# Values by seven products in the second layer of an attention and gated-unit kernel

## The chip, the cores and the metric

The kernel runs on one core of one Trainium2 chip. The metric is the time on the device in microseconds (us); the median over several executions counts. The engines are TensorE (PE, with its weight loads as PEld), VectorE (DVE), ScalarE (ACT), GpSimd (POOL) and SyncE (SP), which here only issues DMAs.

## The reference

Two layers, each a multi-head attention block and a gated linear unit, with the same weights in both. 2048 tokens, 448 features, 16 heads of 28, 1792 hidden features.

```python
def _A_ref(x, wqkv, wo):
    qkv = (x @ wqkv).reshape(B, S, 3, H, Dh).transpose(2, 0, 3, 1, 4)
    q, k, v = qkv[0], qkv[1], qkv[2]
    scores = einsum("bhqd,bhkd->bhqk", q, k) * (Dh ** -0.5)
    p = softmax(scores)
    o = einsum("bhqk,bhkd->bhqd", p, v)
    return o.transpose(0, 2, 1, 3).reshape(B, S, D) @ wo

def _B_ref(x, w_gate, w_up, w_down):
    return einsum("bsf,fd->bsd", sigmoid(x @ w_gate) * (x @ w_up), w_down)

x = A_x
x = x + _A_ref(_layernorm(x), A_wqkv, A_wo)
x = x + _B_ref(_layernorm(x), B_w_gate, B_w_up, B_w_down)
x = x + _A_ref(_layernorm(x), A_wqkv, A_wo)
x = x + _B_ref(_layernorm(x), B_w_gate, B_w_up, B_w_down)
```

## The kernel before, in words

Each layer runs four stages in a row: queries, keys and values (`project`), attention (`attend`), the output projection and the gated unit. The 2048 tokens are four blocks of 512, and a block is four tiles of 128. Numbers in single precision are split into a high and a low half-precision part, so that one exact product is three half-precision ones. The order on every engine is the order of the program text, for each engine by itself; waits are semaphores that the language puts in.

**Seven products.** In the second layer a block of activations stands in two halves each way, and products of 2 by 2 halves are made with seven products in place of eight: the activations' sums and differences lie in `blk.wide` (four operands) and `blk.short` (three, or four where the block keeps the eighth), the weights' sums in packs of 28 planes. Product k of operand k is five matmuls for k below 4 and six from 4 on. Products 0, 2, 3 and 5 are added up in one bank of PSUM (the chain), which is read after each of them; 1, 6 and 4 go to another bank (the side). Queries and keys (`qk_sums`) and the gate (`gate_and_up`) are made in this way. `split_sums` makes the 28 planes of a weight: four sums (`add_up`), four scaled high parts and four low parts on VectorE, then small copies on GpSimd.

**Values.** `vals` makes the values of a block tile by tile: `values_product` is 11 matmuls of 448 columns with the tile of activations as weights, and ScalarE or VectorE copies the bank out. In the second layer the order is: queries and keys of block 3 (`qk_sums(3, ...)`), values of block 2 (`vals(2, ...)`), values of tiles 0 and 1 of block 3, then a branch, tile 2 of block 3, and the first scores of attention. Tile 3 of block 3 is made between the first groups of scores (`last_values`).

**The guard and the branch.** `guard_of_norms` makes for each head a bound on its scores from the norms' maxima (`peaks`): VectorE, a root on GpSimd (L1245), and a scaled row of 2048 on VectorE that reads a cleared tile (`zero`, cleared at L1233). Two rows, the guard and the zeros, are stored to `g_scr` (L1249, L1250). `worst_of_heads` turns the bounds with a matmul (L1254) and compares the worst with a limit; all engines load the flag (L1262) and branch (L1263). The branch not taken holds a slow form (`true_maxima`). Behind it SP loads the guard of head 0 from `g_scr` (L801), which the first scores (L1559) read.

**Attention.** `attend` scores three units (128 keys by 512 queries) at a time into three banks (`score`), ScalarE makes the exponentials of the three in one instruction (L1574), and `mix` multiplies them with the values (L1609) some groups later. A few units of each head are scored aside (`score_aside`): VectorE makes their exponentials with a polynomial (L1584 to L1592). All aside scores of a head use the same bank of PSUM, so one waits until VectorE has read the one before. In the first layer `Prepare`, from step 4 on, reads the other weights, measures and splits them on VectorE and stores the parts (L1442), all DMAs on GpSimd's queue. At step 2 `keep` stores the split weights of queries, keys and values on SP's queue (L752).

**Buffers.** Large tiles in SBUF come from 19 equal buffers (`Slots`, `big`): `get` takes the one that has been free longest, `put` hands it back behind the others. The new user's first write waits until all uses of the old tile are over. `big.ring(6)` takes six for the exponentials.

```python
heads[0].load_guard()
heads[1].load()
heads[1].load_guard()
vals(3, blks[3], {}, [2], 0 if layer == 0 else 7)
```

These four lines stand behind the branch.

Of the kernel before, what the change touches and what calls it, by code (L numbers as in the profile page):

```python
# [59 lines left out]
DN = D // 2  # L60

# [66 lines left out]
def interleaved_layers(ctx: ExitStack, tc: tile.TileContext, x_in, wqkv, wo, w_gate, w_up,  # L128
# [92 lines left out]
    def load_rows(dst, src, c0, n, queue=nc.sync, second=None):  # L221

        for a, b in ((0, 2), (2, 3)) if second else ((0, 3),):
            (second if a else queue).dma_start(
                dst[:, a:b, :], src[a * P:b * P, c0:c0 + n].rearrange("(s p) n -> p s n", p=P))
        for r in (0, 64):
            (second or queue).dma_start(dst[r:r + 64, 3, :], src[384:448, c0:c0 + n])
# [30 lines left out]
    def add_up(v):  # L258

        s12, s34 = [qrt.get("sums", [P, 2, 2, P]) for _ in range(2)]  # L260
        l11, l12, l21, l22 = v[:, 0:2, 0], v[:, 2:4, 0], v[:, 0:2, 1], v[:, 2:4, 1]
        for to, a, b, op in ((s12[:, 0], l21, l22, ALU.add),
                             (s12[:, 1], s12[:, 0], l11, ALU.subtract),
                             (s34[:, 0], l11, l21, ALU.subtract),
                             (s34[:, 1], l12, s12[:, 1], ALU.subtract)):
            nc.vector.tensor_tensor(to, a, b, op=op)
        return s12, s34
# [383 lines left out]
    def of_halves(pm, w, blk, k, first):  # L651


        if k < 4:
            x = blk.wide[:, k]
            high, low, both = w(2 * k + 1), w(2 * k + 15), w(2 * k + 14)
            terms = [(high, x[:, 0, 1]), (high, x[:, 1, 1]), (low, x[:, 0, 1]),
                     (w(2 * k) if k else both, x[:, 0, 0]), (both, x[:, 1, 0])]
        else:
            x = blk.short[:, k - 4]  # L660
            terms = [(w(SHORT[k - 4][i]), x[:, j, 1 - t])
                     for t in range(2) for i, j in ((t, 0), (t, 1), (2 + t, 0))]
        for i, (a, x) in enumerate(terms):
            nc.tensor.matmul(pm, a, x, start=(first and i == 0),  # L664
                             stop=(i == len(terms) - 1), skip_group_check=True)

    def by_tokens(pm, hi, lo, tail, w, kts=range(4)):

        for kt in kts:
            if kt == 3:  # L670
                nc.tensor.matmul(pm, tail, w[:, 0, 3, :], start=False, stop=False)
                nc.tensor.matmul(pm, tail, w[:, 1, 3, :], start=False, stop=True)
                continue
            nc.tensor.matmul(pm, hi(kt), w[:, 0, kt, :], start=(kt == 0), stop=False)  # L674
            nc.tensor.matmul(pm, hi(kt), w[:, 1, kt, :], start=False, stop=False)  # L675
            nc.tensor.matmul(pm, lo(kt), w[:, 0, kt, :], start=False, stop=False)  # L676
# [3 lines left out]
    v_parts = dpool.tile([P, 2, 4, D], F16, name="v_parts")  # L680
    o_parts = dpool.tile([P, 2, 4, D], F16, name="o_parts")
# [5 lines left out]
    class WeightsQKV:  # L687
# [9 lines left out]
        def read(self, j):  # L697
            self.raw.append(big.get("wraw", [P, 4, D]))
            load_rows(self.raw[j], wqkv, j * D, D, second=None if j else nc.scalar)
# [45 lines left out]
        def split_v(self):  # L745
            for kts in (slice(0, 2), slice(2, 4)):
                scaled_split(self.v[:, 0, kts], self.v[:, 1, kts], self.raw[2][:, kts], 2)
            big.put(*self.raw)
# [12 lines left out]
        def load_rest(self):  # L761
# [3 lines left out]
            for i in range(2):  # L765
                nc.sync.dma_start(self.alone[i][:, 0:3], qk_parts[i, :, 0:3, c])
                r = slice(64 * i, 64 * i + 64)
                nc.sync.dma_start(self.alone[0][r, 3], qk_parts[i, r, 3, c])
                nc.sync.dma_start(self.v_tail[r], v_parts[r, i, 3])
# [51 lines left out]
    def project(layer, wq, begun):  # L821
# [10 lines left out]
        evac = [0]  # L832

# [271 lines left out]
        def values_product(pv, blk, j, kts=range(4)):  # L1105
            t = slice(j * P, (j + 1) * P)
            if blk.halves:
                c = slice(j % 2 * P, j % 2 * P + P)
                for s in kts:
# [7 lines left out]
                    for n, (i, w) in enumerate(((0, 0), (0, 1), (1, 0))):  # L1117
                        nc.tensor.matmul(pv[:, 0:D], x[:, i], wq.v[:, w, PLACES[r], :],  # L1118
# [3 lines left out]
                      blk.tail[:, t], wq.v, kts)  # L1122

        def vals(b, blk, after, tiles=range(TB), at=None, begun=None, banks=None):
# [14 lines left out]
            if tiles[-1] == TB - 1:  # L1139
                blk.drop()  # L1140

# [58 lines left out]
        else:  # L1200
            b2.clear()
            ones_of_values()
            b3.apart = True
# [11 lines left out]
                          None, True)  # L1215
            fin = qk_sums(3, b3, {}, fin)
# [14 lines left out]
        def guard_tiles():  # L1231
            tiles = [big.get(n, [H, S], F16) for n in ("guard", "zero")]
            nc.gpsimd.memset(tiles[1], 0.0)  # L1233
            return tiles

        guard_early = guard_tiles() if layer > 0 else None

        def guard_of_norms():
# [9 lines left out]
            queue = nc.gpsimd if guard_early else nc.sync  # L1248
            queue.dma_start(g_scr[:, 0, :], guard)  # L1249
            queue.dma_start(g_scr[:, 1, :], zero)  # L1250
# [8 lines left out]
        vals(2, blks[2], {layer: guard_of_norms, 3: worst_of_heads})  # L1259
        nc.scalar.activation(warm, warm, AF.Exp)  # L1260
        vals(3, blks[3], {}, range(2))
# [10 lines left out]
        vals(3, blks[3], {}, [2], 0 if layer == 0 else 7)  # L1272
# [258 lines left out]
    def attend(layer, values, heads, last_values, gate, wq):  # L1531
# [153 lines left out]
        begun = last_values()  # L1685

# [5 lines left out]
        for g in range(2, groups + 3):  # L1692
            more(g)
            if g == 2:
                last_values(begun)
            x = g - 2.25
# [621 lines left out]
```

## Time and profile before

| | |
|---|---|
| median of 3 runs | 1869.21 us (1868.77 to 1869.33) |
| profiled execution | 1869.45 us, span of its instructions 1867.7 us |
| busy | PE 100%, PEld 76%, DVE 78%, ACT 75%, POOL 16% of the span |
| second layer's values of blocks 2 and 3 | from 1021.78 us on; first scores at 1037.46 us |
| first layer's first scores | 116.51 us |

Rows of the timeline give start and duration in us, engine, line, operation, output and inputs, shapes and how often; in brackets the idle time before and what ended it. A window's row gives for a stretch its length, the busy time (and instructions) of PE, PEld, DVE, ACT and POOL, the granted TensorE clock, the busy share of the DMA engines and GB/s. A matmul's end is modelled, so its pace is read from the starts.

### The profile page before, as it was taken

To read this page: it belongs to the slowest core of one execution; us is meant where nothing else is said; L and a number is where in the kernel's file an instruction comes from. 1 tells how busy PE (TensorE), PEld (TensorE's weight loads), DVE (VectorE), ACT (ScalarE), POOL (GpSimd) and SP (SyncE) were. 2 spreads that over 40 slices of the span, in tenths; PEclk is the share of its full clock that TensorE was granted. 3 is DMA by queue.
4 is the path that set the end of the run, shared out by engine and by line. 5 is a ranking of instruction groups with operands and counts; after the bars stand their busy time and mean duration, and the time that the engine had idled before them with its cause. 6 is when DMAs were issued, how large, how long until landed. Compare 5 with 4: busy or idle time off the path is not lost. (4 is left out here: it accounts for less than half of the span.)

```text
span 1867.7 us, 57157 instructions
## 1 busy us (share of the span) xinstructions
PE 1861.4 (100%) x24479; PEld 1416.1 (76%) x24479; DVE 1462.4 (78%) x2933; ACT 1404.2 (75%) x1865; POOL 306.4 (16%) x582
## 2 busy tenths in 40 slices
PE   9999999999999999999999999999999999999999
PEld 4455566656565899999987568888877668999999
DVE  7748898998997888788877477777777688887764
ACT  6569999999993655555567899999999746555541
POOL 3001123453412111212122000000000031121110
PEclk9999999999999999999999999999999999999999
DMA  7674454454433866757764322122120258677653
GB/s 265 182 214 130 131 160 128 125 156 113 136 129 86 288 211 229 244 204 257 243 187 109 88 52 52 27 53 52 30 50 14 79 165 264 210 249 239 235 201 144
DMA packets 114885, 286.24 MB, mean 153 GB/s; under 512 B 15134, under 2 KB 68878, under 8 KB 114496
## 3 DMA queue, kind: packets, MB, share of 16 engines
q0 software_dynamic: 35088, 174.86, 27.8%
q1 hardware_dynamic: 78384, 106.27, 20.3%
q8 instruction: 194, 3.18, 0.7%
q10 hardware_dynamic: 1152, 1.38, 0.3%
q14 instruction: 67, 0.55, 0.1%
HBM read 218.20 MB, written 54.29 MB: 146 GB/s over the span
## 5 line engine op out<-in xcount | busy, mean ns | idle before, releaser
L1574 ACT ACTIVATE prob_s<-sc 128x1536 f32<-128x1536 f32 (+1 forms) x657 | 888.1, 1484 | 5.9 <-PE sc L1559 3.0
L1609 PE MATMUL acc<-prob_s,val_s 128*32 128x256 f32 (+3 forms) x7708 | 587.2, 384 | 0.0
L1559 PE MATMUL sc<-qp_s 114*32 114x512 f16 x7868 | 571.3, 379 | 0.0
L1559 PEld LDWEIGHTS <-qp_s 114*32 114x32 f16 x8192 | 309.9, 96 | 168.8 <-issue 70.8
L1609 PEld LDWEIGHTS acc<-prob_s,val_s 128*32 128x32 f32 x7708 | 314.1, 110 | 100.3 <-issue 9.2
L1944 PE MATMUL dnp<-dn_s,hparts_s 128*128 128x224 f16 x2184 | 245.8, 259 | 0.0
L664 PEld LDWEIGHTS <-gue_s 128*128 128x128 f16 x2240 | 218.8, 98 | 24.5 <-PE op L1738 0.7
L1944 PEld LDWEIGHTS <-hparts_s 128*128 128x128 f16 x2184 | 210.2, 98 | 5.1
L664 PEld LDWEIGHTS <-gul_s 128*128 128x128 f16 x2016 | 197.0, 98 | 19.9
L664 PE MATMUL chain<-xwide_s,gue_s 128*128 128x256 f16 x1680 | 210.9, 273 | 0.0
L1589 DVE SCALAR_TENSOR_TENSOR power_q<-power_q,expo_q 128x512 f32<-128x512 f32 x243 | 168.2, 692 | 8.3
L664 PE MATMUL side<-xshort_s,gul_s 128*128 128x256 f16 x1344 | 165.0, 273 | 0.0
L2017 ACT COPY one_q<-chain 128x256 f32<-128x256 f32 x224 | 83.1, 372 | 105.4 <-PE chain L664 104.6
L2033 DVE TENSOR_TENSOR one_q<-side,one_q 128x512 f32<-128x512 f32 x112 | 74.3, 689 | 39.1 <-PE side L664 38.8
L1638 DVE STREAM_TRANSPOSE oturned_q<-acc 128x512 f32<-128x512 f32 x32 | 23.0, 717 | 98.4 <-PE acc L1609 98.2
L2044 ACT ACTIVATE one_q<-one_q 128x512 f32<-128x512 f32 x56 | 35.3, 630 | 79.8 <-DVE one_q L2033 79.8
L1609 PE MATMUL acc<-power_q,val_s 128*32 128x256 f32 (+3 forms) x300 | 94.2, 396 | 0.0
L1584 DVE TENSOR_SCALAR expo_q<-aside,base 128x512 f32<-128x512 f32 x81 | 60.6, 748 | 40.5 <-PE aside L1559 40.1
L587 POOL TENSOR_SCALAR rs<-mv 128x1 f32<-128x1 f32 x8 | 1.5, 191 | 505.8 <-DVE mv L585 505.8
L664 PE MATMUL chain<-xshort_s,gul_s 128*128 128x256 f16 x672 | 82.5, 273 | 0.0
L1902 DVE TENSOR_TENSOR hparts_s<-hsums_q,hparts_s 128x256 f16<-128x256 f32 (+1 forms) x152 | 71.3, 519 | 11.1 <-ACT hparts_s L1898 11.1
L664 PE MATMUL side<-xwide_s,gue_s 128*128 128x256 f16 x560 | 79.4, 273 | 0.0
(273 smaller groups left out, 2559.0 us busy)
## 6 DMA issues: line engine op xcount, KB each, us to landing
gue_s<-gu_early POOLq DMA_DIRECT2D x52, 960.0 KB, 5.3
gul_s<-gu_late POOLq DMA_DIRECT2D x52, 768.0 KB, 4.7
dn_s<-dn_parts POOLq DMA_DIRECT2D x42, 784.0 KB, 6.7
qp_s<-qk_scr SPq DMA_DIRECT2D x96, 224.0 KB
xt_scr<-xs_s SPq DMA_DIRECT2D x48, 224.0 KB
xraw_s<-xt_scr SPq DMA_DIRECT2D x12, 768.0 KB
qk_scr<-qkhl_q SPq DMA_DIRECT2D x28, 256.0 KB
qp_s<-qk_scr SPq DMA_DIRECT2D x64, 112.0 KB
```

What stands on the lines that cost most here:

```text
L664: nc.tensor.matmul(pm, a, x, start=(first and i == 0), stop=(i == len(terms) - 1), skip_group_check=True)
L1559: nc.tensor.matmul(ps[32 * j:32 * j + 32, :], hd.k[:, keys], hd.q[:, qb * W:(qb + 1) * W], start=True, stop=True, tile_position=(0, 32 * j))
L1574: nc.scalar.activation(prob[:, 0:n, :], ps[:, 0:n, :], AF.Exp, scale=exp_scale)
L1584: nc.vector.tensor_scalar(y, ps, base2[:, 0:1], -116.0, op0=ALU.mult, op1=ALU.max)
L1589: nc.vector.scalar_tensor_tensor(p, p, c[k], y, op0=ALU.add, op1=ALU.mult)
L1609: nc.tensor.matmul(acc[qb * VC:(qb + 1) * VC, s], v[:, kc % TB, h, :], probs[c * NB + qb][:, s], start=(kc == 0 and a == 0), stop=(kc == N ...
L1638: nc.vector.transpose(turned.rearrange("p b c -> p (b c)"), acc)
L1902: nc.vector.tensor_tensor(to[:, :, 1], a, to[:, :, 0], op=ALU.subtract)
L1944: nc.tensor.matmul(pm, a[:, x, t], w[:, p, y], start=(begin and n == 0 and (j == 0 or alone)), stop=(n == 2), skip_group_check=True)
L2017: nc.scalar.copy(to, pm)
L2033: nc.vector.tensor_tensor(one[m], side[m], one[m], op=ALU.add)
L2044: nc.scalar.activation(out, v, AF.Sigmoid, scale=gate_scale)
```

## The change

In the second layer the values of block 2, and those of tiles 0 and 2 of block 3, are made by the seven products (class `Values`): a group is two tiles (s picks the first or the second of each half), the activations are the weights of the matmul, and the weights' sums move, 224 columns at a time. Block 2 has two groups, run in turn step by step (`by_sevens`), block 3 one. Tile 1 of block 3 is made first of all, in the old way. The guard is made after the second step of block 2, the flag after the second step of block 3; the step 2 of block 3 stands ahead of the branch, its steps 3 to 6 behind it.

The sums of the values' weights are made in the first layer as attention begins: `split_values` for each half of the columns, with 112 columns a plane, and four stores each. For this the raw weights stay in their buffer, with the rows of the short last part put first (`tail=0`) and zeros behind them. `load_products` loads the sums at the second layer's start into two buffers, on GpSimd's queue.

The zeros are stored as soon as they are cleared: in the second layer ahead of the queries and keys of block 3, in the first just ahead of the guard.

```diff
+    vs_early = dpool.tile([P, 2, EARLY, DV], F16, name="vs_early")
+    vs_late = dpool.tile([P, 2, LATE, DV], F16, name="vs_late")
...
         def split_v(self):
             for kts in (slice(0, 2), slice(2, 4)):
                 scaled_split(self.v[:, 0, kts], self.v[:, 1, kts], self.raw[2][:, kts], 2)
-            big.put(*self.raw)
+            big.put(*self.raw[0:2])
+            nc.gpsimd.memset(self.raw[2][64:P, 0, :], 0.0)
+
+        def split_values(self, j):
+
+            t = big.get("vpack", [P, N_SUMS, DV], F16)
+            v = self.raw[2].rearrange("p s (z h n) -> p s z h n", z=2, h=2)[:, :, :, j]
+            split_sums(t, v, up[:, 2:3])
+            for to, a, b in ((vs_early[:, j, 0:7], 1, 8), (vs_early[:, j, 7:EARLY], 14, 22),
+                             (vs_late[:, j, 0:6], 8, 14), (vs_late[:, j, 6:LATE], 22, 28)):
+                nc.gpsimd.dma_start(to, t[:, a:b])
+            big.put(t)
+            if j:
+                big.put(self.raw[2])
+
+        def load_products(self):
+            self.vs = [big.get("vse", [P, 2, EARLY, DV], F16),
+                       big.get("vsl", [P, 2, LATE, DV], F16)]
+            for t, a in zip(self.vs, (vs_early, vs_late)):
+                nc.gpsimd.dma_start(t, a)
...
+        def guard_tiles():
+            tiles = [big.get(n, [H, S], F16) for n in ("guard", "zero")]
+            nc.gpsimd.memset(tiles[1], 0.0)
+            (nc.gpsimd if layer > 0 else nc.sync).dma_start(g_scr[:, 1, :], tiles[1])
+            return tiles
...
+        class Values:
+
+            def __init__(self, b, blk, s, banks):
+                self.b, self.blk, self.s = b, blk, s
+                chain, side = [bank(i, n) for i, n in zip(banks, ("vchain", "vside"))]
+                self.chain, self.side = chain[:, 0:DN], (side[:, 0:DN], side[:, DN:2 * DN])
+
+            def product(self, k, pm):
+                c = slice(self.s * P, self.s * P + P)
+                pm = pm.rearrange("p (j n) -> p j n", j=2)
+                terms = terms_of_halves(wq.part, self.blk, k)
+                for i, (a, x) in enumerate(terms):
+                    nc.tensor.matmul(pm, x[:, c], a, start=(k < 2 and i == 0),
+                                     stop=(i == len(terms) - 1), skip_group_check=True)
+
+            def on_chain(self, k, z, t):
+                self.product(k, self.chain)
+                nc.scalar.activation(self.to(z, t), self.of(self.chain), AF.Copy, scale=PS)
+
+            def plus(self, i, z, t):
+                v = self.to(z, t)
+                nc.vector.scalar_tensor_tensor(v, self.of(self.side[i]), PS, v, op0=ALU.mult,
+                                               op1=ALU.add)
+
+            def do(self, k):
+                if k in (0, 2, 3, 5):
+                    self.on_chain(k, *{0: (0, 0), 2: (0, 1), 3: (1, 1), 5: (1, 0)}[k])
+                    if k == 3:
+                        self.plus(0, 1, 1)
+                else:
+                    self.product(k, self.side[int(k == 4)])
+                    if k == 4:
+                        self.plus(1, 0, 0)
+                    if k == 6:
+                        self.plus(0, 0, 1)
+
+        def by_sevens(b, blk, after):
+            groups = [Values(b, blk, s, ((0, 1), (2, 3))[s]) for s in range(2)]
+            for k in (0, 1, 2, 4, 3, 5, 6):
+                for g in groups:
+                    g.do(k)
+                for do in after.get(k, ()):
+                    do()
+            blk.drop()
...
             ones_of_values()
+            wq.load_products()
...
+            guard_early = guard_tiles()
             fin = qk_sums(3, b3, {}, fin)
...
-            queue = nc.gpsimd if guard_early else nc.sync
-            queue.dma_start(g_scr[:, 0, :], guard)
-            queue.dma_start(g_scr[:, 1, :], zero)
+            (nc.gpsimd if guard_early else nc.sync).dma_start(g_scr[:, 0, :], guard)
...
-        vals(2, blks[2], {layer: guard_of_norms, 3: worst_of_heads})
-        nc.scalar.activation(warm, warm, AF.Exp)
-        vals(3, blks[3], {}, range(2))
+        if layer == 0:
+            vals(2, blks[2], {0: guard_of_norms, 3: worst_of_heads})
+            nc.scalar.activation(warm, warm, AF.Exp)
+            vals(3, blks[3], {}, range(2))
+        else:
+            vals(3, b3, {}, [1], banks={1: 4})
+            by_sevens(2, b2, {1: [guard_of_norms]})
+            group = Values(3, b3, 0, (6, 7))
+            group.do(0)
+            nc.scalar.activation(warm, warm, AF.Exp)
+            group.do(1)
+            worst_of_heads()
+            group.do(2)
...
-        vals(3, blks[3], {}, [2], 0 if layer == 0 else 7)
+        if layer == 0:
+            vals(3, blks[3], {}, [2], 0)
+        else:
+            for k in (3, 4, 5, 6):
+                group.do(k)
+            big.put(*wq.vs)
...
         begun = last_values()
+        if layer == 0:
+            wq.split_values(0)
...
             if g == 2:
                 last_values(begun)
+                if layer == 0:
+                    wq.split_values(1)
```

65 lines of the change are left out of this document (39 added, 26 removed).

## The prediction, made before the result was known

> **What bounds the kernel now.** I read the totals of the page, then the windows and the timeline around the two stages that the change touches: the start of the first layer's attention, and the second layer's values up to its first scores.
>
> ```profile
> span 1867.7 us, 57157 instructions
> PE 1861.4 (100%) x24479; PEld 1416.1 (76%) x24479; DVE 1462.4 (78%) x2933; ACT 1404.2 (75%) x1865; POOL 306.4 (16%) x582
> 124.00:134.00 10.00, 10.00 (x192) 5.78 (x188) 5.81 (x10) 10.00 (x9) 0.00 (x0) 1.00 0.98 336
> 200.00:250.00 50.00, 50.00 (x916) 29.27 (x911) 43.00 (x80) 50.00 (x38) 8.06 (x12) 1.00 0.49 129
> 1026.00:1037.00 11.00, 10.85 (x71) 5.52 (x70) 2.14 (x9) 4.21 (x7) 3.78 (x5) 1.00 0.63 158
> ```
>
> TensorE is busy all the time at full clock (1.00). In the first layer's attention ScalarE is full as well: 38 exponentials in 50 us, one each 1.32 us. So a stop of TensorE there costs time once ScalarE's lead, at most one exponential, is used up. The values (1026 to 1037) are TensorE's alone: VectorE 2.14 and ScalarE 4.21 of 11 us.
>
> **The change, part by part: TensorE's saving.** Old values: 11 products of 448 columns a tile.
>
> ```profile
> 1021.78 0.73 PE L1118 MATMUL vp<-wv_s,xwide_s 128*128 128x448 f16 x3
> 1023.86 0.73 PE L1118 MATMUL vp<-wv_s,xwide_s 128*128 128x448 f16 x3
> 1835.21 29.34 PE dnp L1944 x306
> L1944 PEld LDWEIGHTS <-hparts_s 128*128 128x128 f16 x2184 | 210.2, 98 | 5.1
> ```
>
> From one tile's start to the next are 2.08 us, 0.189 us a product. The new ones have 224 columns, and the last products of the kernel, of that size with a load of weights each, take 29.34/306 = 0.0959 us. Six tiles, 66 products, 12.47 us, become three groups of 38 (four steps of five, three of six): 114, 10.93 us. TensorE saves 1.54 us. The Trainium skill ("TensorE: Matmul & The Clock Gate", LDWEIGHTS) gives a load as its columns over 1.2 in ns, 107 ns for 128; were the load the pace, 114 would take 12.2 us and 0.3 us would be saved. The loads' 98 ns and the pace of 95.9 ns here speak for the larger saving.
>
> **What the saving meets.** After the values of block 3's first two tiles comes a branch on a flag, and behind it the guard's load for head 0, which the first scores need. The change moves the flag's product later.
>
> ```profile
> 1026.42 0.73 PE L1118 MATMUL vp<-wv_s,xshort_s 128*128 128x448 f16 x3
> 1030.68 0.20 PE L1254 MATMUL bounds<-ident,bnd 16*1 16x16 f32 x2
> 1031.19 0.20 DVE L1256 TENSOR_SCALAR flag<-worst,back 1x1 int32<-1x1 f32 x1
> L1263 PEldq COMPARE_BRANCH  x1: 367/367/367, 1032.2 to 1032.2; - x1
> L1263 DVEq COMPARE_BRANCH  x1: 74/74/74, 1032.1 to 1032.1; - x1
> L1263 DVEq EVENT_SEMAPHORE  x1: 21/21/21, 1032.6 to 1032.6; - x1
> 1033.94 0.30 SPq L801 DMA_DIRECT2D qp_s<-g_scr  x1
> 1037.46 1.48 PE L1559 MATMUL sc<-qp_s 114*32 114x512 f16 x24
> 110.16 0.20 DVE L1256 TENSOR_SCALAR flag<-worst,back 1x1 int32<-1x1 f32 x1
> 112.54 0.27 SPq L801 DMA_DIRECT2D qp_s<-g_scr  x1
> DMA to landing us min/median/max: 2.2/2.6/5.4
> 1031.35 1.28 ACT L1260 ACT_TABLE_LOAD   x1
> ```
>
> Before, the flag was there at 1031.39, with 22 products still to run on TensorE, so the branch hid behind them. I run the new order from the same start. One old tile ends at 1023.86; steps 0 and 1 of block 2 (20 products, 1.92) at 1025.78; the norms, whose squares are as late as before, let TensorE go on at 1026.42; five more steps, 56 products, 5.37 us, plus 0.3 us (an estimate) for two copies that the running sum must wait for: 1032.1. Steps 0 and 1 of block 3: 1033.05. Only then comes the flag's product, 2.37 us later than at 1030.68; the flag is written at 1033.76. Only step 2 (0.5 us) is left in front of the branch.
> - TensorE: its branch ended 1.2 us after the flag (1032.2 + 0.37), VectorE took 0.45 us from branch to next instruction; together 1.6 us, so it goes on at 1035.4. Steps 3 to 6, 23 products, 2.2 us, and 0.1 for a copy: scores at 1037.7, 0.24 us later than 1037.46. The table load now stands between the copies of steps 0 and 2 (about 1033.1 to 1034.6) and ends ahead of step 3.
> - SP: the guard's load was issued 2.55 us after the flag in this layer and 2.18 us in the first; now 1035.94 to 1036.31. Its landing isn't in the trace: at least 2.2 us by the quickest landing seen (256 KB stores), at most 3.52 us, since the scores began 3.52 us after it. So scores can start at 1038.1 to 1039.8. I take 1038.5, nearer the quick end, for it is 8 KB on a queue with little before it.
>
> So attention starts 1.0 us later, though TensorE had 1.54 us less to do: **+1.0**, with the ends -1.5 (flag and load are no limit) and +2.4.
>
> The zeros stored sooner remove what waited beside the flag:
>
> ```profile
> 1026.40 1.79 POOL L1233 MEMSET zero_s<- 16x2048 f16 x1
> 1028.16 0.58 POOL L1245 TENSOR_TENSOR bnd<-bnd,half 16x1 f32<-16x1 f32 x1
> 1030.38 0.51 POOL L1250 DMA_DIRECT2D g_scr<-zero_s  x1
> 1015.09 1.47 POOL L951 DMA_DIRECT2D qk_scr<-qkhl_q  x2 [3.08 <-DVE qkhl_q L945]
> ```
>
> The zeros landed about 3.5 us after 1030.38, at 1033.9, level with SP's branch. Without them the guard's own store is there at about 1033, but SP now waits for the flag until 1036: nothing gained. The 1.8 us of clearing moves into POOL's waits of 3 us: nothing lost. In the first layer the zeros change places with the guard on SP, ahead of the branch that ends there at 112.54: nothing.
>
> **The sums of the weights, as the first attention begins.** Two splits of 112 columns are put on VectorE, with copies and four stores each on POOL. The same work on 128 columns stands later in the trace.
>
> ```profile
> 309.61 0.42 DVE L266 TENSOR_TENSOR sums_q<-raws_s 128x256 f32<-128x256 f32 x1
> 315.03 0.22 DVE L289 TENSOR_TENSOR pack_s<-pack_s 64x128 f16<-64x128 f16 x1
> 315.06 0.34 POOL L288 COPY pack_s<-pack_s 64x128 f16<-64x128 f16 x1 [7.35 <-DVE pack_s L275]
> 317.79 1.10 POOL L1442 DMA_DIRECT2D gu_late<-pack_s  x2
> 116.62 0.62 DVE L1138 TENSOR_SCALAR val_s<-vp 128x448 f32<-128x448 f32 x1 [6.26 <-PE vp L672]
> 124.02 0.39 PE L1559 MATMUL aside<-qp_s 114*32 114x512 f16 x4
> 124.46 0.75 DVE L1584 TENSOR_SCALAR expo_q<-aside,base 128x512 f32<-128x512 f32 x1 [2.75 <-PE aside L1559]
> 129.68 0.69 DVE L1592 SCALAR_TENSOR_TENSOR power_q<-power_q,whole_q 128x512 f32<-128x512 f32 x1
> 133.41 0.40 PE L1559 MATMUL aside<-qp_s 114*32 114x512 f16 x4
> 139.28 0.27 PE L1609 MATMUL acc<-power_q,val_s 128*32 128x128 f32 x1
> 114.86 0.59 POOL L1408 DMA_DIRECT2D raw_s<-in_B_w_gate_dram  x1 [8.11 <-ACT val_s L1136]
> 116.61 0.54 POOL L1408 DMA_DIRECT2D raw_s<-in_B_w_up_dram  x1
> 123.60 0.83 SPq L752 DMA_DIRECT2D qk_parts<-wqk_s  x2
> DMA to landing us min/median/max: 7.0/9.4/13.3
> ```
>
> A split took 5.64 us (309.61 to 315.25), POOL's copies and issues 3.8 us more. With 112 columns about 5.1. VectorE is idle here, but for the copies of two value tiles and two exponentials aside of 5.9 us. First split: 117.24 to 122.35. The last tile's copy: 123.0, just ahead of the aside scores at 124.02 that need its bank. Second split: alone it would end at 128.1, and aside scores at 133.41, which need VectorE to have read the first ones (0.8 us), would lose nothing.
>
> But the second split gets the first one's buffer. Large buffers are handed out oldest free first. With the raw weights held, eight are free when the branch is passed (its 16 takes and returns turn the queue of eight twice round), six go to the ring, two are left. The first split takes the older, that of the zeros, and returns it behind the other; head 2 takes the other; the last block's buffer comes in behind; so the second split takes the zeros' again. A buffer is handed on whole, so the split's first scaled part waits until all four stores of the first have landed. They are issued from 123.85 to 125.45, 0.77 MB, while SP stores 2.7 MB of weights and the DMA engines are 98% busy. The nearest rows are the four reads of 448 KB that POOL issued from 114.86 to 116.61: the last landed 13.3 us on, 1.8 MB in 15 us, 119 GB/s. At that pace the stores are down 6.5 us after 123.85, at 130.35. Behind it come 3.75 us of split and 0.8 of the first exponential: 134.9, against 133.41: TensorE stands for 1.5 us (for the time by which the landing is past 128.85). Off that half of ScalarE's lead, 0.65: **+0.85**. The ends: quickest landing 2.2 us (127.7, no stall: 0), slowest 13.3 us (138.8, stall 9.9: +9.2). The exponential itself would be ready 5.9 us after the split, ahead of its use at 139.28 moved by the stall. What VectorE is then behind, it makes up in its idle 4.3 of 10 us below:
>
> ```profile
> 144.00:154.00 10.00, 10.00 (x189) 5.76 (x185) 5.71 (x11) 10.00 (x9) 1.07 (x2) 1.00 0.49 178
> ```
>
> The Trainium skill ("DMA: Bandwidth & Descriptors", Anatomy of one DMA) gives a POOL store 2.0 us and its bytes at 436 GB/s: 2.4 us for the last 172 KB, landed at 127.9, no stall, a sum of +1.0 alone. The contended rows of 7.0 to 13.3 us speak against it here.
>
> **At nothing.** Twelve copies on ScalarE and nine sums on VectorE take the place of six copies; the engines are free for them (4.21 and 2.14 of 11 us above), and where the running sum waits for one I counted it. Loading the sums (1.5 MB, two POOL issues at the second layer's start) has all of that stage's queries and keys before its first use; POOL waits there for the same last products as its clearing of the values, just before it. Other places of the value weights' rows: the same DMAs and products.
>
> **The sum.** +1.0 + 0.85 = 1.9 us. The profiled execution took 1869.45 us, 1.75 around its span of 1867.7, and lies 0.24 above the median of 1869.21; on the median, 1871.1 us.
>
> **The rivals.**
> - *Slower (23%).* The place is the second split's wait. It decides from a last landing at 132.3 on, 6.8 us after its issue: 132.3 - 128.85 - 0.65 + 1.0 = 3.8 us, above 0.2%. For it: no read of POOL's landed below 7.0 us there. Against it: those were twice as large, and they are gone in the new order. At 135 it gives +6.5, 1875.7.
> - *The split is hidden (25%).* Landing before 128.85; the flag's path alone stays: 1870.2. For it: POOL's queue is empty and the quickest landing is 2.2 us.
> - *Faster (7%).* The flag is no limit, the split hidden: -1.5 us, 1867.7; the zeros and the earlier power then count. Against it: 0.5 us of work before the branch where there were 4.2. This is still within 0.2%.
> - *The weight load is the pace (3%).* At the loads' own 98 ns the 86 products ahead of the flag take 0.2 us more: 1871.3. At the page's 107 ns it would be 0.95 us and 1872.1. Against it: 306 products with a load each at 95.9 ns.
>
> **How the numbers follow.** My case, both terms at about their sizes, has 42%: 1870.2 to 1872.9, 1871.1 the likeliest. The range takes in the hidden split and about half of the slower and faster cases: 1868.4 to 1875.2. A measurement of this kernel can tell about 0.2%, 3.7 us, from no change. Of the faster case nearly nothing passes that bound: 3%; slower by more: 23%; within: 74%.
>
> **What would show it.** After: 114 products of 224 columns near 0.096 us; the flag written near 1033.8 by the old start, about 12 us after the values begin; the guard's load 2.2 to 2.6 us behind it, and a gap of TensorE before the first scores. In the first layer a wait of VectorE inside the second split for the sums' stores, and of TensorE at the second aside scores. The prediction is wrong if the scores come less than 15.7 us after the values begin (as before), or if VectorE doesn't wait there and the kernel is slower all the same.

## The result, and the profile after

The changed kernel takes 1879.3 us (median of 6 runs, 1878.81 to 1879.63) against 1869.35 us before (6 runs on the same chip): the ratio is 1.0053, with an interval of 1.004 to 1.0066. It is 9.95 us slower; 1871.1 us were forecast, and a range up to 1875.2. The profiled execution took 1879.28 us.

The totals on the page of the changed kernel, in the columns of those shown for the kernel before:

```profile
span 1877.5 us, 57326 instructions
PE 1862.7 (99%) x24527; PEld 1344.8 (72%) x24527; DVE 1475.9 (79%) x2967; ACT 1405.3 (75%) x1872; POOL 316.2 (17%) x599
```

The span has grown by 9.8 us and TensorE's busy time by 1.3 only: TensorE stands still somewhere. Its waits, summed over the whole span (engine, group, line, what it waited for; us in total, times, longest):

```profile
PE aside L1662 <- DVE expo_q L1687: 5.7, 1, 5.7
...
PE vchain L1198 <- ACT val_s L1209: 1.0, 1, 1.0
PE vside L1198 <- DVE val_s L1213: 0.9, 1, 0.9
...
PE vp L681 <- DVE wv_s L253: 0.3, 1, 0.3
```

None of these four waits is in the kernel before. The largest lies in the first layer's attention; the timeline around it (start, duration, engine, line, operation, and in brackets the idle time ahead with what ended it):

```profile
122.55 0.21 DVE L292 TENSOR_TENSOR vpack_s<-vpack_s 64x112 f16<-64x112 f16 x1
123.63 0.97 SPq L789 DMA_DIRECT2D v_parts<-wv_s  x1
124.21 1.14 POOL L767 DMA_DIRECT2D vs_early<-vpack_s  x2
125.34 1.07 POOL L767 DMA_DIRECT2D vs_late<-vpack_s  x2
135.13 0.34 DVE L275 TENSOR_SCALAR vpack_s<-wraw_s,up 128x224 f16<-128x224 f32 x1 [10.02 <-DMA vs_late<-vpack_s]
138.98 0.75 DVE L1687 TENSOR_SCALAR expo_q<-aside,base 128x512 f32<-128x512 f32 x1
139.78 0.62 PE L1662 MATMUL aside<-qp_s 114*32 114x512 f16 x4 [5.73 <-DVE expo_q L1687]
```

This is the forecast chain at another size. The first split ends at 122.76; VectorE reaches the second split's first scaled part and waits 10.02 us for the first one's stores, whose last lands at 135.0, nine us after its issue. Split and exponential follow, and the second aside scores start at 139.78 instead of 133.41. In the chain of work that ended last (start, duration, engine or transfer, how many) this store stands with 9.13 us:

```profile
125.87 9.13 DMA vs_late<-vpack_s
```

Behind the stop the windows show something that the prediction did not have (the second last columns: granted clock, DMA share, GB/s):

```profile
120.00:132.00 12.00, 12.00 (x217) 6.46 (x209) 4.98 (x12) 11.67 (x10) 3.58 (x7) 1.00 0.98 336
132.00:136.00 4.00, 2.06 (x44) 1.01 (x37) 0.87 (x3) 3.85 (x3) 0.00 (x0) 1.00 0.86 248
136.00:140.00 4.00, 0.21 (x4) 0.16 (x7) 3.90 (x9) 0.00 (x0) 1.13 (x3) 0.85 0.37 82
140.00:144.00 4.00, 4.00 (x40) 1.75 (x36) 3.83 (x6) 0.93 (x1) 3.47 (x7) 0.50 0.64 204
144.00:148.00 4.00, 4.00 (x64) 2.04 (x60) 3.83 (x8) 2.89 (x3) 1.27 (x2) 0.80 0.92 310
```

TensorE comes back at half clock, 0.50 from 140 to 144, and does 40 products there where it does some 80 at 1.00. The end of the second head in the two kernels' timelines (before, then after):

```profile
177.27 0.72 DVE L1638 STREAM_TRANSPOSE oturned_q<-acc 128x512 f32<-128x512 f32 x1 [2.02 <-PE acc L1609]
```

```profile
186.42 0.72 DVE L1741 STREAM_TRANSPOSE oturned_q<-acc 128x512 f32<-128x512 f32 x1 [1.95 <-PE acc L1712]
```

The aside scores were 6.37 us late, the head's end is 9.15 us late: the half clock cost 2.78 us. From there to the second layer's values nothing changes (1030.92 against 1021.78, 9.14). In the second layer:

```profile
1030.92 0.73 PE L1162 MATMUL vp<-wv_s,xwide_s 128*128 128x448 f16 x3
1033.00 1.12 PE L1198 MATMUL vchain<-vse_s,xwide_s 128*128 128x224 f16 x10
1033.96 1.12 PE L1198 MATMUL vside<-vse_s,xwide_s 128*128 128x224 f16 x10
1042.11 1.28 ACT L1356 ACT_TABLE_LOAD   x1
1042.62 0.20 DVE L1344 TENSOR_SCALAR flag<-worst,back 1x1 int32<-1x1 f32 x1
1043.52 0.34 ACT L1209 ACTIVATE val_s<-vchain 128x224 f32<-128x224 f32 x1
1043.91 0.64 PE L1198 MATMUL vchain<-vse_s,xwide_s 128*128 128x224 f16 x5 [1.01 <-ACT val_s L1209]
1044.94 0.30 SPq L837 DMA_DIRECT2D qp_s<-g_scr  x1
1045.41 0.73 PE L1198 MATMUL vside<-vsl_s,xshort_s 128*128 128x224 f16 x6 [0.87 <-DVE val_s L1213]
1046.63 0.74 PE L1198 MATMUL vside<-vsl_s,xshort_s 128*128 128x224 f16 x6
1047.30 1.48 PE L1662 MATMUL sc<-qp_s 114*32 114x512 f16 x24
```

The view puts a wait down to what came last. Most of the 1.01 us is TensorE's own branch on the flag, which stands between step 2 and step 3 (line, queue and operation, duration in ns, start):

```profile
L1361 PEldq COMPARE_BRANCH  x1: 367/367/367, 1043.3 to 1043.3; - x1
```

It ended near 1043.7. ScalarE's copy, which stood behind the table load, was done at 1043.86 and added at most 0.2 us.

From the first value product to the first scores are 16.38 us, 15.68 before: +0.70. And 0.46 us are lost at the start, where block 0's values in the first layer meet the other order of the weights' rows:

```profile
28.86 2.21 DVE L253 SCALAR_TENSOR_TENSOR wv_s<-wraw_s,up,wv_s 128x896 f16<-128x896 f32 x2
31.12 0.35 PE L681 MATMUL vp<-wv_s,xhl_s 128*128 128x448 f16 x1 [0.34 <-DVE wv_s L253]
```

The first scores of that layer start at 116.97, 116.51 before. The whole: 0.46 + (6.37 - 0.46 = 5.91) + 2.78 + 0.70 = 9.85 us, against 9.84 us by which the second layer's first scores are late (1047.30 against 1037.46).

### The profile page after: what moved, and what is told of

Read it like the earlier page. It is cut to its first block, busy times and chain, and to the rows that moved or that the text cites. A ratio compares the mean times of both kernels' runs of the same rounds, so it can differ in the third digit from the quotient of the medians.

```text
span 1877.5 us, 57326 instructions
## 1 busy us (share of the span) xinstructions
PE 1862.7 (99%) x24527; PEld 1344.8 (72%) x24527; DVE 1475.9 (79%) x2967; ACT 1405.3 (75%) x1872; POOL 316.2 (17%) x599
## 4 chain that ended last, share of the span: by engine, by line
PE 92%; DMA 1%; DVE 0%; POOL 0%; ACT 0%; issue 0%; SPq 0%; DVEq 0%; ACTq 0%
PE acc L1712 23%; PE sc L1662 22%; PE chain L669 15%; PE side L669 12%; PE dnp L2051 11%; PE op L680 1%; PE op L682 1%; PE op L681 1%; PE aside L1662 1%; PE vp L1162 1%; PE alone L1067 1%; DMA vs_late<-vpack_s 0%; DMA qp_s<-qk_scr 0%; PE dnp L2099 0%; PE op L1841 0%; PE dnp L2101 0%
## 5 line engine op out<-in xcount | busy, mean ns | idle before, releaser
L1712 PE MATMUL acc<-prob_s,val_s 128*32 128x256 f32 (+3 forms) x7708 | 571.3, 384 | 0.0
L1662 PE MATMUL sc<-qp_s 114*32 114x512 f16 x7868 | 554.3, 380 | 0.0
L1662 PEld LDWEIGHTS <-qp_s 114*32 114x32 f16 x8192 | 273.6, 96 | 208.9 <-issue 94.1
L1712 PEld LDWEIGHTS acc<-prob_s,val_s 128*32 128x32 f32 x7708 | 272.8, 110 | 145.3 <-issue 15.2
```

The costliest lines, as they stand in the source:

```text
L1662: nc.tensor.matmul(ps[32 * j:32 * j + 32, :], hd.k[:, keys], hd.q[:, qb * W:(qb + 1) * W], start=True, stop=True, tile_position=(0, 32 * j))
L1712: nc.tensor.matmul(acc[qb * VC:(qb + 1) * VC, s], v[:, kc % TB, h, :], probs[c * NB + qb][:, s], start=(kc == 0 and a == 0), stop=(kc == N ...
```

## The experiments

Each was timed against the kernel before on its chip, which took 1869.5 us each time (medians 1869.49 to 1869.54).

**Is the shared buffer the loss?** Two buffers: the first pack's is handed back with the second's.

```
-            big.put(t)
             if j:
-                big.put(self.raw[2])
+                big.put(self.first_pack, t, self.raw[2])
+            else:
+                self.first_pack = t
```

> The changed kernel, but the first split's buffer is handed back only with the second's, so that the second split takes another one; the work is the same. Theory (the wait for the buffer stops TensorE 5.9 us, and the half clock that follows costs 2.85 us more): VectorE's wait of 10.02 us inside the second split, the stop and the low clock all go, and first layer's head 0 ends 8.7 us sooner: 1879.3 - 8.75 = 1870.5 us. Rival (the split's work on VectorE, or the traffic of its stores, delays the aside scores, whatever the buffer): the second split would still end past 133 us and the time stay above 1875 us.

Measured: 1871.47 us, ratio 1.001 (1.000 to 1.002): 7.8 of the 9.95 us are back. VectorE waits for no store, and the second aside scores start at 134.19. Of the remaining 2 us, 0.46 and 0.70 are the two terms above. Its profiled execution, which took 1872.96 us and so 1.5 more than the median, shows one more in the second layer:

```profile
1036.00:1040.00 4.00, 3.13 (x20) 2.42 (x18) 0.78 (x2) 0.67 (x2) 0.00 (x0) 0.68 0.40 112
```

Its two short waits of 1.01 and 0.87 us lie there as in the changed kernel, and here the clock fell behind them: 17.89 us from values to scores instead of 16.38. No trace shows what the executions near the median lost beside the two terms, some 0.8 us.

**The split without the products.** The changed kernel with the second layer's values as before; the sums are packed and stored, and not read.

```
-            wq.load_products()
...
-            vals(3, b3, {}, [1], banks={1: 4})
-            by_sevens(2, b2, {1: [guard_of_norms]})
...
+            vals(2, b2, {1: guard_of_norms, 3: worst_of_heads})
+            vals(3, b3, {}, range(2))
```

> The changed kernel with the first layer's part and the zeros' sooner store alone: the second layer's values are made the old way, tile by tile in the old order, and the sums are stored but neither loaded nor used. Theory (the seven products cost 0.70 us net, the rest is the first layer's): 1879.3 - 0.7 = 1878.6 us, scores 15.7 us after the values begin. Rival (the loads of the sums or the buffers they hold cost something elsewhere, or the products gain more than the later flag loses): below 1878 us, or above 1879.3 us.

Measured: 1878.27 us. The stop (5.71 us) and the half clock are there without one of the new products; these account for about 1 us of the loss by the medians, 0.7 by the profiles (15.69 us from values to scores here).

**Why did the stores land so late?** First SyncE's weight stores (2.7 MB) were put one key tile later (`c == 3` for `c == 2` ahead of `wq.keep()`).

> The changed kernel with one edit: SyncE's stores of the split weights (2.7 MB, issued at 122.75 and 123.63 us) come one key tile later, about 127.5 to 128.5 us, so behind the issue of the first pack's four stores (124.21 to 126.4 us). The buffer is still shared. Theory: those stores landed 9 us after their issue because they shared the DMA engines with the 2.7 MB; without it the last one lands near 130, the second split is held till then, TensorE stands for about 1 us, the clock stays 1.00, and the time is about 1871.5 us from the first layer's other terms and the flag plus that 1 us: 1872.5 us (1871.5 to 1874). Rival, that GpSimd's queue itself takes 9 us for these stores: 1879.3 us as before, stop 5.7 us. The later stores may hold up the next head's loads: then TensorE waits for them near 140 us.

Measured: 1879.97 us, and it tells nothing on the theory: SyncE has nothing between the two places, so its issue stayed where it was.

```profile
122.70 0.83 SPq L788 DMA_DIRECT2D qk_parts<-wqk_s  x2
```

Then they were put ahead of the first layer's branch, the buffers handed back where they were.

```
         def keep(self):
-            for i in range(2):
-                nc.sync.dma_start(qk_parts[i], self.qk[i])
-            nc.sync.dma_start(v_parts, self.v)
             big.put(*self.qk, self.v)
+        def store(self):  # the three lines taken out of keep
...
+        if layer == 0:
+            wq.store()
         loose = nc.values_load(flag[0:1, 0:1], min_val=0, max_val=1)
```

> The changed kernel with one edit: SyncE issues the stores of the first layer's split weights (2.7 MB) ahead of the branch, at about 108.5 us, instead of at 122.75 us; the buffers are handed back where they were. So no weight store is under way when GpSimd issues the first pack's four stores (about 124.2 to 126.4 us). Theory: those landed 9 us after their issue because they shared the DMA engines with the 2.7 MB; now the last lands by about 129 us, 3 us after its issue, TensorE stands for at most 1 us before the second aside scores, the clock stays 1.00 there, and the time is 1872 us (1871.2 to 1874.5; the upper end if head 0's guard load at 113 us comes late behind the weights). Rival, that GpSimd's queue takes 9 us for these stores whatever else runs: the stop of 5.7 us and the half clock stay, 1879.3 us.

Measured: 1876.12 us (1874.84 to 1877.49). The DMA issues from 118 to 132 us, last number the median from issue to landing, of the changed kernel and of this one:

```profile
vs_late<-vpack_s POOLq DMA_DIRECT2D x2, 168.0 KB, 9.1
vs_early<-vpack_s POOLq DMA_DIRECT2D x1, 224.0 KB, 9.4
```

```profile
vs_late<-vpack_s POOLq DMA_DIRECT2D x2, 168.0 KB, 5.7
vs_early<-vpack_s POOLq DMA_DIRECT2D x1, 224.0 KB, 5.8
```

So the weight stores made the difference of 3.4 us; GpSimd's queue alone doesn't take nine. What is left has to do with other transfers too: the second pack's stores, of the same sizes, landed 2.2 to 2.7 us after their issue in the changed kernel (from 140.25 us on, after the DMA engines had stood nearly idle from 138 to 141), and 5.2 to 6.8 us after it with two buffers, where the DMA engines were 99 to 100% busy from 128 to 140 us. TensorE has no wait at the second aside scores, and the clock stays 1.00 from 120 to 164 us. What the theory's 1872 us lacked is on the other side of the move, in the timeline of SyncE:

```profile
109.10 0.97 SPq L792 DMA_DIRECT2D v_parts<-wv_s  x1
117.89 0.28 SPq L839 DMA_DIRECT2D qp_s<-g_scr  x1
```

Head 0's guard load is issued at 117.89 (112.99 in the changed kernel), and the first scores come at 119.55, 2.6 us later. TensorE stands 2.71 us ahead of these scores, and the clock stays 1.00 there too. VectorE still waits 5.44 us inside the second split, until 131.6, where the theory had the last landing at 129. Without TensorE's delay, a landing past 128.85 + 0.46 = 129.3 would stop it; so some 2.3 us of stop are hidden by the delay. In the second layer this execution had a half clock as well (17.69 us).

**Is the half clock the idleness, and what does it cost?** 24 products with a zero operand, adding nothing to head 0's sum, were put where TensorE stands still: in the changed kernel, and in the one with the split alone.

```
             ps = bank(1 - u // (NT * NB) % 2, "aside")
+            if layer == 0 and u == (15 * NB + 1):
+                for _ in range(24):
+                    nc.tensor.matmul(accs[0], zeros[:, 0:P], zeros, start=False, stop=False,
+                                     skip_group_check=True)
```

> The changed kernel, with 24 products of zeros (512 columns, 0.216 us each, 5.2 us in all) added to head 0's accumulator just ahead of the second aside scores of the first layer: TensorE works through the stop, which stays as long. They add nothing to the result. Theory (the clock falls because TensorE stood still): no window below full clock, the stop stays (aside scores near 139.8 us), and the 2.85 us go: 1879.3 - 2.85 = 1876.4 us. Rival (the clock falls for another reason, such as VectorE and the DMAs working at once): 0.5 still granted from 140 us on, 1879.3 us.

> The changed kernel with the second layer's values as before, and 24 products with a zero operand ahead of the second aside scores, so that they fill TensorE's 5.7 us of standing still (the earlier try at this put them behind the stop). They add zeros to head 0's sum. Clock theory: granted clock 1.00 from 128 to 152 us, the aside scores where they were, and the 2.85 us of half clock come back: 1878.3 - 2.85 = 1875.4 us (1874.9 to 1876.3). Rival, that the half clock costs nothing because ScalarE and VectorE pace those scores: 1878.3 us.

Measured: 1884.21 us and 1877.38 us. In the first, the changed kernel, the granted clock is 1.00 from 120 to 152 us, the second aside scores start at 139.68, 6.27 us late, and the second head ends 6.27 us late, where it was 9.15:

```profile
183.54 0.72 DVE L1746 STREAM_TRANSPOSE oturned_q<-acc 128x512 f32<-128x512 f32 x1 [1.46 <-PE acc L1717]
```

So in the first layer the 2.8 us came back. In the second:

```profile
134.48 5.35 PE L1676 MATMUL acc<-zeros_q 128*128 128x512 f16 x24
139.76 0.40 PE L1654 MATMUL aside<-qp_s 114*32 114x512 f16 x4
```

```profile
140.00:144.00 4.00, 4.00 (x76) 2.07 (x72) 3.83 (x6) 2.42 (x2) 3.44 (x7) 1.00 0.64 205
```

```profile
183.56 0.72 DVE L1738 STREAM_TRANSPOSE oturned_q<-acc 128x512 f32<-128x512 f32 x1 [1.19 <-PE acc L1709]
```

The scores come as late as with the split alone (139.76 and 140.08), at full clock, and the second head ends 6.29 us late for scores 6.35 us late. With the split alone:

```profile
185.82 0.72 DVE L1733 STREAM_TRANSPOSE oturned_q<-acc 128x512 f32<-128x512 f32 x1 [1.97 <-PE acc L1704]
```

There it ended 8.55 us late for scores 6.67 us late. So the half clock is the idleness's, and about the same stop cost 1.9 us more there and 2.8 in the changed kernel. The windows of 1 us tell why: TensorE worked at half clock for 5.8 us in the changed kernel (139.78 to 145.6) and for 4.0 with the split alone (140.08 to 144.1), and about half of such a time was lost (2.8 and 1.9). And of ScalarE's lead nothing came back: 6.35 us of delay stayed 6.29, and 6.27 stayed 6.27.

Not all of the gain reaches the end: 0.9 us with the split alone, by the medians, and in the changed kernel more than all of it is lost again. With the split alone 1.8 us are lost again up to the second layer's values (8.09 us late there), with waits that its sibling doesn't have:

```profile
PE side L669 <- DMA xwide_s<-xshort_s: 1.0, 1, 1.0
...
PE chain L669 <- ACT one_q L2124: 0.5, 1, 0.5
```

In the other, TensorE comes late out of the second layer's branch, and a half clock follows; from values to scores it takes 20.96 us instead of 16.38:

```profile
1044.84 0.75 PE L1198 MATMUL vchain<-vse_s,xwide_s 128*128 128x224 f16 x5 [3.92 <-PEq L1361]
```

What it waited for is TensorE's own sequencer, not ScalarE's copy, which was done at 1041.88. The branch instruction itself took 3.36 us, where it was 0.37 in the changed kernel:

```profile
L1361 PEldq COMPARE_BRANCH  x1: 3358/3358/3358, 1041.3 to 1041.3; - x1
```

Two runs with other numbers of products went after this.

> The changed kernel with 20 zero products instead of 24 in the stop: 4.5 of its 5.9 us filled, 1.4 us left idle. Clock theory: 1.00 from 128 to 152 us in the first layer. What is open is the second layer's branch, where with 24 products TensorE's sequencer was 3.9 us late and a half clock followed. If that comes from where the branch's code lies in TensorE's instruction stream, eight instructions fewer may take it away: 1876.5 us; if any such products bring it, 1883 to 1884 us.

> The changed kernel with 8 zero products in the stop instead of 24 or 20. They fill 1.8 of 5.9 us, so 4.1 us stay idle and the half clock is to be expected as in the changed kernel: 1879.3 us, if nothing else happens. The open point is TensorE's sequencer at the second layer's branch, 3.9 us late with 24 and with 20 products, not with none. If the place of the branch in TensorE's instruction stream sets this, it may be absent here (1879.3 us); if any product more ahead of it brings it, about 3 us and a half clock more, 1885 us.

Measured: 1883.68 us with 20, where the sequencer was again 3.9 us late; 1879.43 us with 8, where it was not (the branch took 0.37 us and the wait is back to 1.01 us). With the split alone and 24 products, where the branch stands behind other instructions, it took 0.37 us as well. So it isn't any product more ahead of the branch; that it is the branch's place in the instruction stream fits, but no run shows it, and it stays open. With 20 products TensorE stood for 1.35 us in the first layer and the clock stayed 1.00, as expected; with 8 it still stood for 3.1 us and the clock fell.

In an earlier run with the split alone the 24 products stood behind the stop, not in it.

> The changed kernel with the second layer's values as before (the packed weights stored and not read), and 24 products with a zero operand put where TensorE stands idle in the second split; they add zeros to head 0's sum. Clock theory: the stop of 5.7 us is filled, the granted clock stays 1.00 behind it, and 2.85 us of the 1878.3 of the same kernel without the products come back: 1875.4 us (1874.9 to 1876.4). Rival, that the half clock costs nothing because VectorE and ScalarE pace those scores anyway: 1878.3 us. If the loss at the flag's branch that the changed kernel with the same products showed (TensorE's sequencer 3.9 us late) comes with these products in any kernel, another 3 us.

Measured: 1884.71 us. The stop was as long as without them, and they took 7.58 us in its half clock instead of 5.35. It says nothing on the theory; its branch took 0.37 us, so the late sequencer doesn't come with these products in any kernel.

**How long a stop?** In the kernel with two buffers VectorE was held by additions of its own behind the second split, nine or twelve.

```
+                    nc.vector.memset(idle, 0.0)
+                    for _ in range(9):
+                        nc.vector.tensor_tensor(idle, idle, idle, op=ALU.add)
```

> The two-buffer kernel (both packs' buffers kept, so no wait for a store) with one clearing and nine additions of 128x512 put on VectorE behind the second split: they hold VectorE as the missing buffer did, for less time, with no transfer in it. TensorE's stop before the second aside scores should be about 2 us. Clock theory: such a stop lies inside one span of the clock's watch, the granted clock stays 1.00 between 128 and 152 us, and the time is the two-buffer kernel's 1871.5 plus 2.0, so 1873.5 us (1872.5 to 1874.5). Rival, that any stop lowers the clock: a half clock behind it as long as in the changed kernel, 2.85 us more, so 1876.3 us.

> The same with twelve additions: a stop of about 4 to 4.5 us, made by VectorE alone. Clock theory: long enough that the granted clock falls to 0.50 for some 5 us behind it, so 1871.5 + 4.3 + 2.85 = 1878.6 us; if the stop happens to lie so that no whole span of the watch is idle, 1875.8 us and a clock of 1.00. Rival, that the half clock came from the stores' traffic and not from the idleness: 1.00 and 1875.8 us always.

Measured: 1875.96 and 1879.28 us. The stops were longer than planned, 3.01 and 5.19 us. The shorter one's clock:

```profile
136.00:140.00 4.00, 2.75 (x32) 1.52 (x35) 3.83 (x7) 0.04 (x1) 0.86 (x3) 0.57 1.05 291
140.00:144.00 4.00, 4.00 (x74) 2.19 (x69) 3.86 (x7) 3.61 (x3) 0.88 (x2) 1.00 0.96 338
```

No store is waited for here, and the clock falls all the same: it is not the transfer. The second head ends 5.12 us late for scores 3.84 us late: 1.3 us for a stop of 3.0. With 5.19 us it is 1.9. Here too it is about half of the time that TensorE worked at half clock, 2.75 and 4.0 us. The first expectation, that a stop this short leaves the clock alone, could not be tried at 2 us and is wrong at 3; the stops of 1.35 and 2.71 us above did leave it at 1.00.

**The flag and the last terms.** With two buffers: the table load behind step 2 of block 2, the flag's product behind step 3 of block 2, and behind the branch the steps in the order 4, 3, 5, 6.

```
-            by_sevens(2, b2, {1: [guard_of_norms]})
+            by_sevens(2, b2, {1: [guard_of_norms], 2: [to_exp], 3: [worst_of_heads]})
...
-            for k in (3, 4, 5, 6):
+            for k in (4, 3, 5, 6):
```

> As with two buffers, and in the second layer the table load stands behind step 2 of block 2 and the flag's product behind its step 3, and behind the branch step 4 of block 3 comes ahead of step 3 as in block 2. Theory (the late flag, the copy behind the table load and the sum that step 4 waits for take back the saving): TensorE has no gap ahead of the first scores, they come 14.3 to 14.6 us after the values begin, where it was 16.38: 1870.5 - 2.0 = 1868.5 us. Rival (the guard's load bounds the scores): the guard is stored 7.4 us after the values begin and lands 3.7 us later, its load could be issued at 11.2 and land at 13.6, so it bounds only if it takes longer: then 1869.5 us or more.

Measured: 1870.1 us, ratio 1.0004 (0.9994 to 1.0013).

```profile
1022.36 0.73 PE L1163 MATMUL vp<-wv_s,xwide_s 128*128 128x448 f16 x3
...
1034.68 0.74 PE L1199 MATMUL vside<-vsl_s,xshort_s 128*128 128x224 f16 x6 [0.32 <-PEq L1360]
...
1036.34 0.73 PE L1199 MATMUL vchain<-vsl_s,xshort_s 128*128 128x224 f16 x6 [0.45 <-ACT val_s L1210]
...
1037.58 1.48 PE L1661 MATMUL sc<-qp_s 114*32 114x512 f16 x24
```

From values to scores are 15.22 us: 0.46 us less than before, not the 1.1 to 1.4 expected. Of the 1.54 us that TensorE saves, 0.77 go to the two waits shown. Here the seven products do gain, and 0.57 us from the first layer takes it away. Then the value weights were also split in pairs that fit the products, those of row tiles 0 and 1 first (`slice(1, 3), slice(0, 4, 3)` for `slice(0, 2), slice(2, 4)`).

> The kernel with two buffers and the flag ahead of the last products of the third block, and the first layer's split of the value weights in another pairing of the row tiles: first the two that block 0's products read first (places 1 and 2), then the others. Theory: TensorE's first value products no longer stop 0.35 us for the second half of the split (31.12 back to 30.66), and the 0.45 us that this cost come back: 1870.1 - 0.45 = 1869.65 us (1869.2 to 1870.1), no difference from before that can be measured. Rival, that the 0.57 us by which its first scores were late come from elsewhere in the first stage: 1870.1 us.

Measured: 1869.91 us, ratio 1.0006 (0.9995 to 1.0017). The wait of the first values is gone from the trace; of the 0.45 us the median shows 0.19, too little to tell. Neither of the last two versions can be told from the kernel before.

Last, the zeros alone, in the kernel before: `guard_tiles()`, with the zeros' store in it, moved ahead of the fourth block's queries and keys.

> The kernel before with one part of the change alone: the guard's zeros are cleared and stored ahead of the fourth block's query and key sums in the second layer, and ahead of the guard in the first. Theory: the zeros were never what SyncE's guard load waited for, so nothing moves: 1869.5 us (1868.9 to 1870.2). Rival, that the earlier clearing holds GpSimd's copies of the last queries and keys: up to 1.8 us more, 1871.3 us.

Measured: 1869.56 us against 1869.54: nothing, as expected.

## Why the prediction was wrong

- **The second split's buffer (+0.85): the step that failed.** That the pack gets the first one's buffer, who waits and where TensorE stops all came as written. The landing was mis-sized: "At that pace the stores are down 6.5 us after 123.85, at 130.35". It was 135.0. The pace came from the reads of GpSimd at 119 GB/s; the stores, 0.77 MB from 124.21 to 135.0, had 71 GB/s, beside the weight stores that shared the engines, and their landings of 8.4 to 9.4 us lay among those of the twice as large reads quoted beside them (7.0 to 13.3). The landings themselves, not bytes over a pace, were the nearest row: 7.0 to 13.3 us behind the issue is 132 to 139. The "slower" rival named this case and its price, 1875.7 us at 135; it should have led.
- **Half clock behind the stop: not in the sum, nor in a rival.** 2.78 us. The row was there to be asked for: every window quoted had TensorE full at 1.00, and none showed what a stop of some microseconds does to it. The Trainium skill ("TensorE: Matmul & The Clock Gate", What's actually happening) has the clock at half after about 3.4 us of idleness, in windows that run free. The stop of 5.7 us agrees; those of 3.0 us, and in some executions of 1.01 and 0.87 us within 2.5, lowered it too, so here the measurement decides.
- **"Off that half of ScalarE's lead, 0.65": wrong.** Nothing came back.
- **"Other places of the value weights' rows: the same DMAs and products": wrong by 0.46 us.** The split runs in two halves, and row tile 1 moved into the second.
- **The flag (+1.0): right, for partly other reasons.** The flag was written 11.90 us after the values began (forecast 11.98), ten products took 0.96 us, and the attention started 0.70 us late. But TensorE and not the guard's load was last: that load went out 2.12 us behind the flag (2.2 to 2.6 forecast) and the scores followed the last product. The load's landing was also taken too long: with the weight stores ahead of the branch the scores start 1.66 us after its issue (117.89 to 119.55), where at least 2.2 us were taken. TensorE's branch ended 0.9 us after the flag and not 1.6, and made some 0.8 of the wait of 1.01 us; ScalarE's table load, which stood ahead of step 2's copy, added at most 0.2. Another 0.87 us went to VectorE's sum of step 3, which step 4's product waits for.
- **The zeros, the first split (5.1 us), the weight load's pace:** as forecast.

## What to carry to other kernels

When a buffer is handed on while a store still reads it, price the wait by landings seen in that stretch of the trace, not by bytes over a pace, and ask which large transfers of other queues start within the same microseconds. Any stop of TensorE of some 3 us or more in a stretch where it is full is to be priced with the half clock behind it (here 1.3 to 2.8 us beside the stop). A wait shown with one cause may have had another nearly as long behind it: what the waiting engine's own queue did in that time is to be read as well. A saving of 1.5 us on an engine ahead of a branch is worth only what is left when the flag's chain, the copies and the sums between the products are laid out in the new order.

## What the runs showed of the hardware that was not expected

- The granted clock fell to half in stops of 3.0 to 5.7 us, 2.3 to 4.7 us after TensorE had stopped, and stayed there until 2.7 to 5.8 us after it came back. About half of that last time is what the half clock cost. It stayed 1.00 behind stops of 1.35 and 2.71 us. Behind two waits of 1.01 and 0.87 us it fell in some executions (0.68 from 1036 to 1040 us in the one shown, 1.3 to 1.5 us more to the scores) and not in others with the same instructions.
- GpSimd's stores of 168 to 224 KB landed 8.4 to 9.4 us after their issue beside 2.7 MB of SyncE's stores, and after 5.3 to 5.8 us without them. The Trainium skill ("DMA: Bandwidth & Descriptors", Anatomy of one DMA) gives 2.0 us and the bytes at 436 GB/s, 2.4 to 2.5 us. The second pack's stores in the changed kernel agree, with 2.2 to 2.7 us; none of the first pack's came near it.
- TensorE's sequencer held the products behind a branch up for 3.92 us with 20 or 24 more products in the changed kernel (its branch took 3.36 us instead of 0.37), and not with 8 or none, nor with 24 in the kernel with the split alone. The cause stays open.
